# Loads of the matrices to be inverted: one DMA per 32 partitions in place of one per 64

## The chip, the cores and the metric

One core of one Trainium2 chip runs the kernel. The metric is the device time of one execution in microseconds (us); lower is better. Before the change the median of three runs is 1321.84 us.

## The reference, cut to what matters

A recurrence over 768 positions (32 pairs of batch and head, state 40 x 40), then two dense stages.

```python
for t in range(S):                                   # S = 768; B, H, D = 4, 8, 40
    y[:, :, t] = einsum('bhd,bhde->bhe', r[t], state)
    Sa = einsum('bhde,bhe->bhd', state, a[t])
    state = state * w[t] - Sa (x) b[t] + v[t] (x) k[t]
x = y as (3072, 320)
x = ((x @ w_a) * (x @ w_b)) @ w_out                  # 320 -> 1536 -> 320
each row of x to one of 8 experts (argmax of a gate): gate * relu(x @ w1[e]) @ w2[e]
```

## The kernel before, in words

The recurrence is worked in 12 chunks of 64 positions. Within a chunk the dependence of each position on the earlier ones is a triangular 64 x 64 matrix for each of the 32 pairs. Its two diagonal 32 x 32 blocks are inverted on VectorE (DVE): 64 small matrices, each held on two partitions (even and odd rows), so that all 128 partitions work at once. The off-diagonal block follows by small matmuls (`t21a`, `t21b`).

**The path of one inversion.** `scores` (L545) makes the matrices by matmuls (L551) of `ablk` and `bk`, ScalarE copies them to `s1` (L559), GpSimd masks them (L561), and SyncE (SP) writes them to a DRAM tile `nd` of shape [2, 32, 32, 32] (L568): diagonal block k, pair s, row j, column t. `tinv` (L602) loads them back into the tile `m` (L613 to L623): partitions 64k to 64k+31 and 64k+32 to 64k+63 get the same 32 matrices of 4 KB each. It then loads the identity into `xt` (L624) and returns 31 pairs of DVE steps, `mul` (L630) and `sub` (L636). At the last one `end` writes `xt` to a DRAM tile `td` (L647) and reads it back into `s1` (L651, L652).

**What sets the order.** PE, DVE, ScalarE and GpSimd run in the order in which the program is written. `phase1` goes through 24 slots for each chunk c and places work of the chunks c, c+1, c+2 and c+3 in them by the table `STEADY`. For chunk c+2: its `bk` is loaded in slot 0 (L471), its `a` in slot 2 (L521, multiplied on GpSimd at L523 and spread into `ablk` at L531), `bk` is scaled on DVE in slot 2 (L541), `scores` stand in slots 7, 8, 16 and 17, `tinv` is called in slot 22, and its DVE steps run in slots 2 to 16 of the next chunk. Slot 0 of a chunk also loads `rblk` (L725) and `r` (L729), which the matmuls at L826 and L844 use. The matmuls of the first dense layer (L1019, tile `pm`) for the chunk before are laid into the odd slots, 16 in each; their products (L1031) go out as `hT` (L1033). Steps that convert 64-bit weights (lines 365 to 388) are mixed between the steps of the inversion.

All these loads and stores are issued by SP, in one order. The loads of the 64-bit weights and of `v` are issued by ScalarE. DMAs of SP and ScalarE take turns with eight completion semaphores, so a DMA waits until the one eight earlier in the program's order has landed.

**Special cases.** The inversions of chunks 0 and 1 are made ahead of the loop. Chunk 1 has its tiles lent by another pool (`room`): there `m` is two halves of 16 rows, which are loaded apart (L616). The chunks 2 to 11 use L621.

Of the kernel before, what the change touches and what calls it, by code (L numbers as in the profile page):

```python
# [22 lines left out]
R = C // 2  # L23
# [109 lines left out]
def phase1(tc, I, cst, drm, psA, psM, ident, hT, mk_ident, wo, xs, span, tiny, down):  # L133
# [61 lines left out]
    while tinv or t1:  # L195
        both += tinv[:1] + t1[:1]
        tinv, t1 = tinv[1:], t1[1:]
# [202 lines left out]
def urow(b, o):  # L400
    return slice(C * (b % 2) + o, C * (b % 2) + o + R)


class Attention:
# [197 lines left out]
    def tinv(self, c, room=None):  # L602


        nc = self.nc
        st = self.st[c]
        if room:
            m, xt = room
        else:
            t = self.p1.tile([128, R, R], F32, tag="m", name=f"m{c}")  # L610
            m = [t[:, R // 2 * h:R // 2 * h + R // 2] for h in range(2)]
            xt = self.p1.tile([128, R // 2, R], F32, tag="xt", name=f"xt{c}")
        for k in range(2):  # L613
            if room:
                for h in range(2):
                    nc.sync.dma_start(  # L616
                        m[h][64 * k:64 * k + 64].rearrange("p j t -> p (j t)"),
                        st["nd"][k, :, R // 2 * h:R // 2 * h + R // 2].rearrange(
                            "s j t -> s (j t)")[None].to_broadcast([2, 32, R * R // 2]))
            else:  # L620
                nc.sync.dma_start(  # L621
                    t[64 * k:64 * k + 64],
                    st["nd"][k].rearrange("s j t -> s (j t)")[None].to_broadcast([2, 32, R * R]))  # L623
        nc.sync.dma_start(xt, self.I["one"].rearrange("p (i t) -> p i t", t=R))  # L624

        def mul(s, box):
            n, rows = R - 1 - s, s // 2 + 1
            tmp = self.p2.tile([128, 136], F32, tag="tmp", name=f"tmp{c}_{s}")[:, :rows * n]
            box.append(tmp.rearrange("p (i t) -> p i t", t=n))
            nc.vector.tensor_tensor(  # L630
                box[0], m[2 * s // R][:, s % (R // 2):s % (R // 2) + 1, s + 1:].to_broadcast([128, rows, n]),
                xt[:, :rows, s:s + 1].to_broadcast([128, rows, n]), op=ALU.mult)

        def sub(s, box):
            rows = s // 2 + 1
            nc.vector.tensor_tensor(  # L636
                xt[:, :rows, s + 1:], xt[:, :rows, s + 1:], box[0], op=ALU.subtract)
            if s == R - 2:
                end()

        def end():
            t0, t1 = self.td[c % 2]
            for k, t in ((0, t0), (1, t1[:, :, R:])):
                tv = t.rearrange("s (i k) t -> k s i t", k=2)
                for q in range(2):
                    p = 64 * k + 32 * q
                    nc.sync.dma_start(tv[q], xt[p:p + 32])  # L647
            for b in range(B):
                s1 = st["s1"][b // 2][:, b % 2]
                ss = slice(8 * b, 8 * b + 8)  # L650
                nc.sync.dma_start(s1[urow(b, 0), :, 0:R], t0[ss].rearrange("s j t -> j s t"))  # L651
                nc.sync.dma_start(s1[urow(b, R)], t1[ss].rearrange("s j t -> j s t"))  # L652

        out = []
        for s in range(R - 1):
            box = []
            out.append(lambda s=s, box=box: mul(s, box))
            out.append(lambda s=s, box=box: sub(s, box))
        return out
# [1122 lines left out]
```

## Time and profile before

| | |
|---|---|
| median of 3 runs | 1321.84 us (1315.72 to 1326.93) |
| the profiled execution: its own time | 1319.37 us |
| the profiled execution: span from first to last instruction | 1317.2 us |
| mean granted TensorE clock | 0.884 of full speed |
| busy: PE, DVE, ScalarE (ACT), GpSimd (POOL) | 1051.8, 704.1, 521.6, 439.3 us |

The span is one execution. Engines overlap, so busy times do not add up to it. "SPq" is the time that SP's queue takes to issue a DMA; when a DMA lands is seen in the chain of waits and in what waits for it. The recurrence runs to about 870 us, the rest is dense work.

### The profile page before, as it was taken

Reading aid. Unit: us, or ns where it says so; the run is one execution under the profiler, and the core shown is the slowest. Engines: PE = TensorE matmul, PEld = TensorE weight load, DVE = VectorE, ACT = ScalarE, POOL = GpSimd, SP = SyncE. Lnnn points to the kernel's source line nnn. Section 1 sums busy time; section 2 is a strip of 40 time slices with the busy share of each in tenths; the row PEclk is TensorE's granted clock in tenths of the full one; section 3 lists DMA queues with packets and bytes.
Section 4 is the critical chain, followed back from the end, with each engine's and each line's share of the span. In section 5 each row is a group of like instructions: output and inputs, shape, how many; then the busy total and the mean of one; then the engine's idle time right before and its main releaser. Section 6 shows DMA issues by size and latency. Waiting matters only on the chain.

```text
span 1317.2 us, 27177 instructions
## 1 busy us (share of the span) xinstructions
PE 1051.8 (80%) x10402; PEld 1005.3 (76%) x10402; DVE 704.1 (53%) x1843; ACT 521.6 (40%) x1229; POOL 439.3 (33%) x464
## 2 busy tenths in 40 slices
PE   2304649788786877779788889999999989999995
PEld 2303639687776866778787879899999989999995
DVE  7488648382846646283848383713366684222221
ACT  3435634343342524344343324343233434445441
POOL 5442533121322312122332222112022255666550
PEclk9655659889897879889897989999799999999998
DMA  7363344446564838454444433318255727454510
GB/s 189 92 163 77 87 100 101 110 100 136 126 120 122 158 105 155 112 133 116 116 102 117 100 89 91 90 53 232 81 175 174 237 82 226 135 161 146 156 44 13
DMA packets 236828, 162.21 MB, mean 123 GB/s; under 512 B 142594, under 2 KB 220115, under 8 KB 236689
## 3 DMA queue, kind: packets, MB, share of 16 engines
q1 hardware_dynamic: 218945, 133.15, 39.3%
q0 software_dynamic: 9808, 15.76, 4.2%
q10 hardware_dynamic: 7936, 11.47, 3.1%
q8 instruction: 84, 1.38, 0.4%
q14 instruction: 55, 0.45, 0.1%
HBM read 107.34 MB, written 44.60 MB: 115 GB/s over the span
## 4 chain that ended last, share of the span: by engine, by line
PE 39%; DMA 25%; DVE 17%; issue 8%; POOL 4%; ACT 4%; SPq 2%; ACTq 0%; POOLq 0%; DVEq 0%
PE pm L1019 10%; PE py L1156 8%; DMA m<-nd 8%; PE dn L1465 5%; PE u L1445 5%; DVE tmp L630 5%; DVE xt L636 4%; DMA wo<-wo 3%; DMA xt<-in_one 3%; DMA bk<-in_bk 2%; PE s1p L551 2%; DMA at<-in_a 2%; POOL s L833 2%; DMA out<-y,ids 1%; PE py L850 1%
## 5 line engine op out<-in xcount | busy, mean ns | idle before, releaser
L630 DVE TENSOR_TENSOR tmp<-m,xt 128x126 f32<-128x126 f32 (+22 forms) x372 | 127.6, 346 | 116.1 <-DMA bk<-in_bk 79.4
L1019 PE MATMUL pm<-xl,wh 128*128 128x256 f32 x576 | 134.7, 317 | 15.5 <-ACT ua L1022 13.2
L551 PE MATMUL s1p<-ablk,bk 120*128 120x192 f32 (+1 forms) x264 | 64.6, 400 | 92.3 <-DMA ablk<-at 58.7
L1031 DVE TENSOR_TENSOR uh<-pm,ua 128x256 f32<-128x256 f32 x144 | 60.5, 420 | 141.5 <-PE pm L1019 93.2
L551 PEld LDWEIGHTS s1p<-ablk,bk 120*128 120x128 f32 x264 | 57.1, 249 | 96.4 <-issue 77.7
L1019 PE MATMUL pm<-xh,wl 128*128 128x256 f32 x576 | 120.8, 293 | 0.0
L1019 PE MATMUL pm<-xh,wh 128*128 128x256 f32 x576 | 119.7, 291 | 0.0
L636 DVE TENSOR_TENSOR xt<-xt,tmp 128x126 f32<-128x126 f32 (+22 forms) x372 | 113.5, 308 | 8.2
L1448 DVE SCALAR_TENSOR_TENSOR hl<-u,hh 128x384 fp32r<-128x384 f32 (+5 forms) x72 | 41.5, 580 | 139.1 <-ACT hh L1447 139.1
L1019 PEld LDWEIGHTS pm<-xl,wh 128*128 128x128 f32 x576 | 93.7, 202 | 19.6 <-ACT ua L1022 14.0
L1019 PEld LDWEIGHTS pm<-xh,wl 128*128 128x128 f32 x576 | 94.7, 202 | 0.0
L1019 PEld LDWEIGHTS pm<-xh,wh 128*128 128x128 f32 x576 | 93.8, 200 | 0.0
L833 POOL TENSOR_SCALAR_AFFINE_SELECT s<-s 64x512 f32<-64x512 f32 x96 | 70.7, 737 | 67.6 <-ACT s L831 63.2
L1156 PE MATMUL py<-wl,hh 128*128 128x328 f32 x288 | 92.5, 321 | 0.6 <-DVE wl L1127 0.6
L1156 PE MATMUL py<-wh,hl 128*128 128x328 f32 x288 | 91.3, 317 | 2.0 <-DVE hl L1146 2.0
L1156 PE MATMUL py<-wh,hh 128*128 128x328 f32 x288 | 91.1, 316 | 0.0
L561 POOL TENSOR_SCALAR_AFFINE_SELECT s<-s 64x512 f32<-64x512 f32 x48 | 37.3, 778 | 150.1 <-ACT s L559 144.8
L826 PE MATMUL p<-rblk,uv 120*128 120x192 f32 (+1 forms) x288 | 61.3, 377 | 30.4 <-DMA rblk<-in_r 29.6
L1022 ACT COPY ua<-pm 128x256 f32<-128x256 f32 x144 | 53.7, 373 | 79.0 <-PE pm L1019 58.8
L1019 PE MATMUL pm<-xl,w 128*128 128x256 f32 x288 | 84.0, 292 | 0.0
L1019 PE MATMUL pm<-xh,w 128*128 128x256 f32 x288 | 83.9, 291 | 0.0
L826 PEld LDWEIGHTS p<-rblk,uv 120*128 120x128 f32 x288 | 58.0, 240 | 32.0 <-issue 31.0
(236 smaller groups left out, 2750.8 us busy)
## 6 DMA issues: line engine op xcount, KB each, us to landing
hT<-uh SPq DMA_DIRECT2D x72, 256.0 KB
hf<-hT SPq DMA_DIRECT2D x36, 512.0 KB
r<-in_moe_w SPq DMA_DIRECT2D x8, 1280.0 KB
r<-in_moe_w SPq DMA_DIRECT2D x8, 1024.0 KB
bk<-in_bk SPq DMA_DIRECT2D x11, 720.0 KB
xs<-zt SPq DMA_DIRECT2D x8, 805.0 KB
m<-nd SPq DMA_DIRECT2D x22, 256.0 KB
at<-in_a SPq DMA_DIRECT2D x24, 180.0 KB
```

The lines of the kernel that those rows point to most:

```text
L551: nc.tensor.matmul(ps[:2 * C, 3 * g * C:(3 * g + n) * C], st["bk5"](b, g), self.ablk[b // 2][:, b % 2, g, 0:n, 0:C], start=True, stop=True)
L630: nc.vector.tensor_tensor(box[0], m[2 * s // R][:, s % (R // 2):s % (R // 2) + 1, s + 1:].to_broadcast([128, rows, n]), xt[:, :rows, s:s + ...
L636: nc.vector.tensor_tensor(xt[:, :rows, s + 1:], xt[:, :rows, s + 1:], box[0], op=ALU.subtract)
L826: nc.tensor.matmul(p2[b][:, 3 * g * C:(3 * g + n) * C], self.cur[b]["uv"][:, 128 * g:128 * g + 128], self.rblk[:, b % 2, g, 0:n, 0:C], sta ...
L833: nc.gpsimd.affine_select(out=s2t[q * C:q * C + C], in_=s2t[q * C:q * C + C], pattern=[[0, 8], [1, C]], base=0, channel_multiplier=-1, com ...
L1019: nc.tensor.matmul(p, l, r, start=(i == 0), stop=(i == len(seq) - 1))
L1022: nc.scalar.copy(a, p)
L1031: nc.vector.tensor_tensor(h[:, f % 2], p, a, op=ALU.mult)
L1156: self.nc.tensor.matmul(py, self.pair[i][l][:, k, s], self.W[r][:, first + k, cols], start=(first + k == 0 and n == 0), stop=(first + k == ...
L1445: nc.tensor.matmul(p, l, r, start=(i == 0), stop=(i == len(seq) - 1))
L1448: nc.vector.scalar_tensor_tensor(out=hl, in0=p, scalar=0.0, in1=hh.bitcast(F32), op0=ALU.max, op1=ALU.subtract)
L1465: nc.tensor.matmul(p, l[:, q], r[:, f], start=(f == 0 and i == 0), stop=(f == len(hs) - 1 and i == 2))
```

## The change

For each diagonal block k, the DMA that filled 64 partitions reads its source through a leading broadcast dimension of 2, that is, as [2, 32, 1024] elements. It becomes two DMAs, q = 0 and 1, that fill 32 partitions each, whose source is [32, 32, 32] without a broadcast. The same bytes reach the same places. For the chunks with L621 there are four DMAs of 128 KB in place of two of 256 KB; for chunk 1 there are eight of 64 KB in place of four of 128 KB.

```diff
         for k in range(2):
-            if room:
-                for h in range(2):
-                    nc.sync.dma_start(
-                        m[h][64 * k:64 * k + 64].rearrange("p j t -> p (j t)"),
-                        st["nd"][k, :, R // 2 * h:R // 2 * h + R // 2].rearrange(
-                            "s j t -> s (j t)")[None].to_broadcast([2, 32, R * R // 2]))
-            else:
-                nc.sync.dma_start(
-                    t[64 * k:64 * k + 64],
-                    st["nd"][k].rearrange("s j t -> s (j t)")[None].to_broadcast([2, 32, R * R]))
+            for q in range(2):
+                p = slice(64 * k + 32 * q, 64 * k + 32 * q + 32)
+                for h in range(2 if room else 0):
+                    nc.sync.dma_start(m[h][p], st["nd"][k, :, R // 2 * h:R // 2 * h + R // 2])
+                if not room:
+                    nc.sync.dma_start(t[p], st["nd"][k])
         nc.sync.dma_start(xt, self.I["one"].rearrange("p (i t) -> p i t", t=R))
```

## Rows read from the trace of the kernel before

**Rows 1.** The page's 40 equal slices of the span: PE's busy tenths.
```profile
PE   2304649788786877779788889999999989999995
```

**Rows 2.** The chain that ended last, its shares of the span by line.
```profile
by line: PE pm L1019 10.2%; PE py L1156 7.8%; DMA m<-nd 7.6%; issue 7.5%; PE dn L1465 5.3%; PE u L1445 5.1%; DVE tmp L630 4.8%; DVE xt L636 3.7%; DMA wo<-wo 3.4%; DMA xt<-in_one 3.1%; DMA bk<-in_bk 2.2%; PE s1p L551 2.1%; DMA at<-in_a 1.6%;
```

**Rows 3.** DMA issues by tile: count and KB each.
```profile
m<-nd SPq DMA_DIRECT2D x22, 256.0 KB
...
m<-nd SPq DMA_DIRECT2D x4, 128.0 KB
```

**Rows 4.** The timeline of SP: start, us, line, what, count.
```profile
385.45 1.25 SPq L621 DMA_DIRECT2D m<-nd  x2
386.75 0.41 SPq L624 DMA_DIRECT2D xt<-in_one  x1
...
387.68 10.11 SPq L725 DMA_DIRECT2D rblk<-in_r  x3
397.89 1.05 SPq L729 DMA_DIRECT2D r<-in_r  x2
400.64 0.32 SPq L471 DMA_DIRECT2D bk<-in_bk  x1
...
426.70 1.24 SPq L725 DMA_DIRECT2D rblk<-in_r  x3
```

**Rows 5.** The chain in order of time, 380 to 415 us: start, us, what.
```profile
384.40 1.69 DMA nd<-s
...
386.16 14.42 DMA m<-nd
...
400.64 5.92 DMA bk<-in_bk
```

**Rows 6.** Busy time by stretch; last three columns: granted clock, DMA share, GB/s.
```profile
386.20:390.00 3.80, 3.80 (x68) 3.47 (x68) 1.41 (x4) 2.64 (x7) 0.00 (x0) 1.00 0.69 179
...
396.00:398.00 2.00, 2.00 (x18) 1.91 (x16) 0.00 (x0) 1.10 (x3) 0.00 (x0) 1.00 0.13 51
...
400.60:406.60 6.00, 3.75 (x12) 3.49 (x12) 0.21 (x2) 0.58 (x1) 0.00 (x0) 0.59 0.82 217
```

**Rows 7.** The timeline of PE, same boundary; in brackets idle time before.
```profile
402.76 3.75 PE L826 MATMUL p<-rblk,uv 120*128 120x192 f32 x12 [4.65 <-DMA rblk<-in_r]
412.94 2.05 PE L551 MATMUL s1p<-ablk,bk 120*128 120x192 f32 x6 [6.43 <-DVE tmp L630]
```

**Rows 8.** The timeline of SP at the first and last of eight such boundaries.
```profile
236.56 1.39 SPq L621 DMA_DIRECT2D m<-nd  x2
...
252.12 0.33 SPq L471 DMA_DIRECT2D bk<-in_bk  x1
...
738.00 1.28 SPq L621 DMA_DIRECT2D m<-nd  x2
...
753.85 0.33 SPq L471 DMA_DIRECT2D bk<-in_bk  x1
```

**Rows 9.** The timeline of PE after the last of them.
```profile
766.39 2.04 PE L551 MATMUL s1p<-ablk,bk 120*128 120x192 f32 x6 [6.32 <-DVE xt L636]
```

**Rows 10.** The timeline of SP at the inversions of chunks 0 and 1.
```profile
44.20 1.17 SPq L621 DMA_DIRECT2D m<-nd  x2
47.45 13.25 SPq L568 DMA_DIRECT2D nd<-s  x8
...
61.88 2.43 SPq L616 DMA_DIRECT2D m<-nd  x4
```

**Rows 11.** The timeline of DVE there.
```profile
59.98 0.19 DVE L630 TENSOR_TENSOR tmp<-m,xt 128x31 f32<-128x31 f32 x1 [13.15 <-DMA m<-nd]
...
75.57 0.38 DVE L630 TENSOR_TENSOR tmp<-m,xt 128x31 f32<-128x31 f32 x2 [4.81 <-DMA m<-nd]
```

**Rows 12.** The chain, 36 to 237 us: the load after the inversion of chunk 2.
```profile
164.54 16.82 DMA w<-in_w
```

**Rows 13.** Waits of SP, 120 to 870 us: us in total, times, longest.
```profile
SPq L568 <- DMA vn<-in_vn: 26.6, 9, 8.1
...
SPq L471 <- DMA m<-nd: 16.4, 9, 3.4
```

## The prediction

> **What bounds the kernel now.** I read the page's slices first, then the chain of waits, then the timelines of SP, PE and DVE around one load of `m`. In the slices PE stands at nine tenths from about the 25th on and mostly at six to eight tenths before [rows 1], so up to some 770 us something else sets the pace. The chain names it: `m<-nd` holds 7.6% of the span, 100 us, and `xt<-in_one`, which is issued right behind it, 3.1%, 41 us [rows 2]. For a load of 512 KB per inversion that is a lot. In the timeline of SP the two DMAs of one inversion are issued from 385.45 [rows 4]; in the chain the second lands 14.42 us after 386.16, whereas the larger `bk` (720 KB) needs 5.92 [rows 5]. The busy times say how the 14 us pass: at 396 to 398 the DMA engines are busy for a share of 0.13, about two of sixteen, at 51 GB/s, where the stretch after has 0.82 and 217 GB/s [rows 6]. Two engines carry the load and the other fourteen wait for work.
>
> What follows suffers too. SP issues `rblk` in three DMAs that take 10.11 us to issue, where the same three take 1.24 later in the chunk [rows 4]: SP is held up behind the full engines. `bk` then waits for `m` itself (nine such waits, 16.4 us in all [rows 13]), as each DMA waits for the one eight earlier. On PE this is 4.65 us of idle time before L826, for `rblk`, and 6.43 us before L551, the scores, which need `bk` and `ablk` [rows 7]. There are eight such boundaries, the first with `m` issued at 236.56, the last at 738.00 [rows 8]; after the last one's scores at 766.39 [rows 9] PE has no gap left to close.
>
> A rule of the Trainium skill ("DMA: Bandwidth & Descriptors", section "Rules for kernel authors") says that a DMA uses at most as many engines as its outermost dimension counts, and names a leading broadcast of c copies as the case that confines it to c; by it the old load has two engines and the new one, with 32 outermost, sixteen. The share of 0.13 agrees for the old load; no row shows the new form.
>
> **The change, part by part.** *Issues.* 22 DMAs become 44, and 4 become 8 [rows 3]: 26 more, at 1.25/2 = 0.62 us each [rows 4], two of them (1.25 us) on the path of an inversion.
>
> *The load itself.* No row shows its new form. Bounds for the landing after the last issue: 1.69 us from below, as the 32 KB of `nd<-s` take, and 14.42 from above, as now; the nearest is `bk` at 720 KB in 5.92 [rows 5], 122 GB/s with its fixed part, which gives 512/122 = 4.2 us. I take 4. It matters little: `m` is wanted by DVE together with `bk`, which comes later.
>
> *What is late next: `bk`.* SP after the first issue of `m` at 385.45: four issues 2.5, `xt` 0.4, one store of `hT` about the same, `rblk` 1.24 [rows 4], `r` 1.05 [rows 4], together 5.6 us, so 391.1. The wait for the DMA eight back now falls on `rblk`, `r` and `bk`, for the four parts of `m`; with a landing 4 us after 388.0 `bk` starts at 392.0 instead of 400.64, that is 8.6 us earlier. Behind that wait stand, on SP, `a` and then `ablk`, for which the scores wait; both move along with `bk`. From the issue of `bk` to the scores it is 412.94 - 400.64 = 12.3 us [rows 4, 7], and that stays. So the scores start at 404.3 instead of 412.94.
>
> *Whether PE is ready.* PE stopped at 402.76 - 4.65 = 398.1 before L826 [rows 7]; with `rblk` there it goes on at once, needs up to 3.75 us and is free at 401.9, still before 404.3. PE's gap shrinks from 11.1 to about 2.5 us, and DVE's steps of the inversion, which stand behind the scaling of `bk`, begin 8.6 us earlier as well. After the scores everything is relative to them, so the boundary's gain is kept.
>
> *The eight boundaries.* From the first issue of `m` to that of `bk` the first boundary takes 15.6 us, the last 15.9 [rows 8], this one 15.2 [rows 4]; the others lie between 14.3 and 15.9. With 6.6 us afterwards the gain is 7.7 to 9.3, 8.5 on average: 8 x 8.5 = 68 us. The load at 801 us belongs to the last inversion, past 766.39, where PE is the bound: 0.
>
> *Chunks 0 and 1.* `m` is issued at 44.20 [rows 10], and DVE is idle for 13.15 us until 59.98 and for 4.81 until 75.57 [rows 11]. With four issues (2.5) and a landing of 3 to 4 us the first start moves to about 50: 10 us won. The eight sends of `nd` behind it take 13.25 us to issue [rows 10]; freed, they end near 54, when chunk 1's scores are masked. Its eight loads take 8 x 0.6 = 4.9 us (2.43 for four [rows 10]) and land near 63. DVE, with its 10.8 us of steps between the two waits, is there at 61, so the second gap shrinks to 2. Together 12.5 us.
>
> *Chunk 2.* Behind its `m` the load of `w`, 366 KB, takes 16.82 us [rows 12], for which ScalarE, then DVE, then PE wait. Half of `bk`'s size should land within `bk`'s 5.92 [rows 5]; less 1.2 for the later issue, 16.8 - 5.9 - 1.2 = 9.7 are won, counted as 10.
>
> *The sum.* 68 + 12.5 + 10 = 90.5 us. The profiled execution took 1319.37 us (its span 1317.2 and 2.2 around it), 2.5 below the median shown and within its three runs: 1319.4 - 90.5 = 1229. A second way: the chain gives `m` and `xt` 141 us [rows 2]; with about 4.5 us left at each of eleven inversions, 141 - 50 = 91.
>
> **The rivals.**
>
> *The whole gap closes.* If `bk` comes sooner, PE's order is what is left: 4.65 + 6.43 = 11.1 us [rows 7] at eight boundaries, 89 us, and 25 for the start: 114 and 1205 us. For it: the 5.92 us of `bk` were measured in a stretch where DMAs had piled up (share 0.82 [rows 6]). Against: its successors pile up with it again.
>
> *The transfers only meet each other.* With `m` out of the way, `m`, `xt`, `hT`, `rblk`, `r` and `bk`, some 2.1 MB, want the engines at once. At the 179 GB/s of the first stretch [rows 6] they need 11.7 us and `bk` lands at 397.9, as forecast; at `bk`'s own 122 GB/s [rows 5] 17.2 us, so `bk` lands at 403.4 instead of 406.6: 3.2 us per boundary, 26, and half of the start, 11: 37 us and 1282. For it: the many short rows of `rblk`. Against: 217 GB/s in the busiest stretch [rows 6].
>
> *The load stays slow.* If what makes it slow is not the number of engines (all copies read the same 128 KB, say), it keeps its 14.4 us, and the added issues put 1.25 us on the path at ten inversions and 2.4 at chunk 1: 14.9 us and 1334, slower. It decides from a landing later than 386.16 + 14.42 - 385.45 = 15.1 us after the first issue [rows 4, 5], which is what the load takes now. Against: the share of 0.13 in DMA engines [rows 6], which a slow source would not confine to two of sixteen.
>
> The same page and section of the Trainium skill advises against splitting one transfer over disjoint halves of the partitions, since both spread over all sixteen engines and run one after the other; where that held for the old load, the change would only add issues, and the time would be that 1334. The 0.13 does not agree with it here.
>
> A wait for a DMA eight back can also hold SP on a transfer that ScalarE issues late: `vn` holds the sends of `nd` nine times, at most 8.1 us [rows 13]. These sends are ahead of `m`, and the two more DMAs come behind them, so I see no new one; each that arose would take up to 8.1 us off the gain at its boundary.
>
> **How the numbers follow.** The forecast of 1229 has a chance of 0.67, with 1212 to 1248 as its own range (7.5 to 10.5 us a boundary); the whole gap 0.12; the meeting transfers 0.14; the slow load 0.07. A measurement of this kernel, whose three runs lie 0.85% apart, tells about 1% from no change. Faster by over 1%: 0.67 + 0.12 + 0.13 = 0.92. Within 1%: half of the slow load and the rest of the third case, 0.05. Slower: 0.03. The range reaches from 1198, a little past the closed gap, to 1268, most of the way to the third case; the slow load and the tails beyond, 0.19 in all, are left out.
>
> **What would show it.** Right: `m<-nd` at 4 us or less in the chain, no stretch with a DMA share near 0.13 after it, three `rblk` issues in 1.3 us, `bk` issued about 6.6 us after the first `m`, idle time before L826 gone and before L551 at 2 to 4 us, and the last scores near 766 - 90 = 676 us. After these scores the remaining work takes as long as before. Wrong: `bk` landing later than 8 us after its issue (the transfers meet), or `m` still at 14 us. The forecast would also fail if the periods between scores were held by something that the load now hides, a chain through PE or ScalarE of less than 8 us of slack.

## The result and the profile after

The changed kernel takes 1227.7 us (median of four runs, 1226.58 to 1231.55) against 1321.9 us before (a median of four as well): a ratio of 0.9295, with a 95% interval of 0.925 to 0.934. The forecast was 1229. The execution that the profile shows took 1231.55 us, its span 1229.8; the mean granted clock is 0.915 (0.884 before).

The page's slices, PE's busy tenths:

```profile
PE   1404779988798887888999899999999999999995
```

PE stands at seven to nine tenths from the fifth slice on and mostly at nine from about the 20th, where it had six to eight for most of the way and nine only from about the 25th [rows 1]. The chain of the page, by line:

```profile
PE pm L1015 15%; PE py L1152 8%; PE u L1441 7%; PE dn L1461 7%; DVE tmp L626 5%; DMA wo<-wo 4%; DVE xt L632 4%; DMA hT<-uh 2%; POOL s L829 2%; PE s1p L551 2%; PE py L846 1%; DMA at<-in_a 1%; DVE bk L541 1%; PE p L822 1%; PE px L752 1%
```

`m<-nd` and `xt<-in_one`, 10.7% together in [rows 2], are no longer among the lines named, and `pm`, which stood at the head before too, goes from 10.2% to 15%. (In the changed kernel L617 and L619 load `m`; all lines past the change have moved up by four: L626 is the old L630, L721 the old L725, L822 the old L826.) The page counts 44 issues of `m` of 128 KB, as the change says.

SP at the boundary that answers to [rows 4], the first issues of `m` at the start, at chunk 2 (with the load of `w`) and at the first boundary, and the sends of chunk 1's `nd` (start, us, line, what, count):

```profile
44.96 2.06 SPq L619 DMA_DIRECT2D m<-nd  x4
...
50.02 6.00 SPq L568 DMA_DIRECT2D nd<-s  x8
...
57.32 6.46 SPq L617 DMA_DIRECT2D m<-nd  x8
...
152.55 1.01 SPq L619 DMA_DIRECT2D m<-nd  x2
154.13 0.34 SPq L462 DMA_DIRECT2D w<-in_w  x1
...
214.46 1.80 SPq L619 DMA_DIRECT2D m<-nd  x4
...
347.55 1.80 SPq L619 DMA_DIRECT2D m<-nd  x4
349.40 0.42 SPq L620 DMA_DIRECT2D xt<-in_one  x1
349.86 0.43 SPq L1029 DMA_DIRECT2D hT<-uh  x1
350.34 1.48 SPq L721 DMA_DIRECT2D rblk<-in_r  x3
351.91 0.93 SPq L725 DMA_DIRECT2D r<-in_r  x2
352.93 0.36 SPq L471 DMA_DIRECT2D bk<-in_bk  x1
```

The three issues of `rblk` take 1.48 us instead of 10.11, and `bk` goes out 5.4 us after `m` instead of 15.2. The load stands in the chain (start, us, what) at the inversion of chunk 0 alone. Before the change it took there, and after it takes:

```profile
44.84 15.04 DMA m<-nd
...
46.38 3.83 DMA m<-nd
```

At the eight boundaries it no longer stands in the chain, so that its landing there is seen only where something else waits for it. `r` does at two of them, 3.7 us in all (SP's waits are shown further below); at the longer one `r` is out 7.7 us after the first issue of `m`, where the old form had landed after 15.1 us [rows 4, 5].

Busy time by stretch at the same boundary (stretch, us, PE, PEld, DVE, ScalarE, GpSimd, then granted clock, DMA share, GB/s):

```profile
347.50:350.00 2.50, 2.50 (x48) 2.27 (x48) 0.58 (x2) 0.86 (x3) 1.00 (x1) 1.00 0.82 230
350.00:353.00 3.00, 3.00 (x62) 2.75 (x59) 0.61 (x2) 2.28 (x6) 0.00 (x0) 1.00 0.93 250
353.00:360.40 7.40, 7.40 (x140) 7.02 (x139) 0.52 (x2) 3.43 (x9) 0.00 (x0) 1.00 0.97 256
```

The stretch at 0.13 [rows 6] is gone: the engines are nearly full until `bk` has landed. ScalarE at the first use of chunk 2's `w`, and DVE, with the wait before it in brackets:

```profile
159.19 0.62 ACT L488 ACTIVATE junk<-w,wlim 120x384 f32<-120x384 f32 x1 [0.16 <-DMA w<-in_w]
```

```profile
51.41 0.19 DVE L626 TENSOR_TENSOR tmp<-m,xt 128x31 f32<-128x31 f32 x1 [3.87 <-DMA m<-nd]
...
65.02 0.40 DVE L626 TENSOR_TENSOR tmp<-m,xt 128x31 f32<-128x31 f32 x2
...
360.45 0.56 DVE L541 TENSOR_TENSOR bk<-bk,suf 120x384 f32<-120x384 f32 x1 [5.99 <-DMA bk<-in_bk]
```

`bk` was issued at 352.93 and is there at 360.4: 7.5 us, where it took 5.92 [rows 5]. PE at this boundary, and at the last scores:

```profile
362.11 1.91 PE L822 MATMUL p<-rblk,uv 120*128 120x192 f32 x12
366.14 1.11 PE L551 MATMUL s1p<-ablk,bk 120*128 120x192 f32 x6 [2.12 <-DMA ablk<-at]
...
681.80 1.11 PE L551 MATMUL s1p<-ablk,bk 120*128 120x192 f32 x6 [1.61 <-DMA ablk<-at]
```

The gap before `rblk`'s matmuls is gone, that before the scores is 2.12 us instead of 6.43 [rows 7], and the last scores start 84.6 us earlier than in [rows 9]. Here both groups of matmuls run at the full clock: 1.91 us for twelve and 1.11 for six, where it was 3.75 and 2.05 [rows 7]. By stretch, the two groups before the change, and both after it (columns as above):

```profile
402.76:406.51 3.75, 3.75 (x12) 3.46 (x12) 0.00 (x0) 0.58 (x1) 0.00 (x0) 0.50 0.96 258
412.94:414.99 2.05, 2.04 (x7) 2.05 (x8) 1.86 (x8) 0.00 (x0) 0.50 (x1) 0.50 0.77 172
...
362.11:367.25 5.14, 3.02 (x22) 2.86 (x21) 5.04 (x11) 1.50 (x3) 4.19 (x6) 1.00 0.26 60
```

The granted clock was 0.50 in both groups before, behind 4.65 and 6.43 us without a matmul, and is 1.00 now. That holds for `rblk`'s twelve at all eight boundaries (1.91 us). The scores' six take 1.11 us at four of them; at three they still take 2.04 to 2.05 us, behind gaps of 4.58 to 5.47 us, as here:

```profile
568.91 2.04 PE L551 MATMUL s1p<-ablk,bk 120*128 120x192 f32 x6 [5.47 <-DMA ablk<-at]
```

### The profile page after: what moved, and what is told of

It is laid out like the page before. It is cut to its first block, busy times and chain, and to the rows that moved or that the text cites. A ratio compares the mean times of both kernels' runs of the same rounds, so it can differ in the third digit from the quotient of the medians.

```text
span 1229.8 us, 27217 instructions
## 1 busy us (share of the span) xinstructions
PE 1035.7 (84%) x10402; PEld 991.2 (81%) x10402; DVE 703.1 (57%) x1843; ACT 523.0 (43%) x1229; POOL 439.1 (36%) x464
## 4 chain that ended last, share of the span: by engine, by line
PE 51%; DVE 18%; DMA 15%; issue 6%; ACT 4%; POOL 4%; SPq 1%; POOLq 0%; ACTq 0%; DVEq 0%
PE pm L1015 15%; PE py L1152 8%; PE u L1441 7%; PE dn L1461 7%; DVE tmp L626 5%; DMA wo<-wo 4%; DVE xt L632 4%; DMA hT<-uh 2%; POOL s L829 2%; PE s1p L551 2%; PE py L846 1%; DMA at<-in_a 1%; DVE bk L541 1%; PE p L822 1%; PE px L752 1%
## 5 line engine op out<-in xcount | busy, mean ns | idle before, releaser
L626 DVE TENSOR_TENSOR tmp<-m,xt 128x126 f32<-128x126 f32 (+22 forms) x372 | 126.3, 342 | 22.5 <-DMA rblk<-in_r 4.4
L551 PE MATMUL s1p<-ablk,bk 120*128 120x192 f32 (+1 forms) x264 | 59.8, 377 | 71.2 <-DMA ablk<-at 42.4
L551 PEld LDWEIGHTS s1p<-ablk,bk 120*128 120x128 f32 x264 | 52.7, 233 | 74.4 <-issue 50.4
L1205 POOL DMA_INDIRECT xs<-xr,si x24 | 28.0, 1168 | 138.5 <-DVE acc L1200 87.2
L994 POOL TENSOR_TENSOR xl<-xf,xh 128x384 fp32r<-128x384 f32 x24 | 24.3, 1011 | 144.8 <-ACT xh L993 121.2
```

Source lines behind the costliest of these rows:

```text
L551: nc.tensor.matmul(ps[:2 * C, 3 * g * C:(3 * g + n) * C], st["bk5"](b, g), self.ablk[b // 2][:, b % 2, g, 0:n, 0:C], start=True, stop=True)
L626: nc.vector.tensor_tensor(box[0], m[2 * s // R][:, s % (R // 2):s % (R // 2) + 1, s + 1:].to_broadcast([128, rows, n]), xt[:, :rows, s:s + ...
```

## The experiments

The theory (A): the old DMA is slow because it runs on two engines, as many as its outermost dimension counts; what is behind it is held up by those two full engines. Against it stand that the broadcast in the source, or the same 4 KB rows being read twice, made it slow, and that what was won came from another order of the queue and not from the engines. All ratios are against the kernel before on the same chip, with the 95% interval.

**The changed kernel once more**, as a measure for the others on the same chip.

> The changed kernel once more, unaltered, for comparison on the same chip with the three beside it: ratio 0.9295 (0.925 to 0.934) to the kernel before.

1226.27 us, a ratio of 0.9313 (0.928 to 0.935): the same gain in a second measurement.

**One engine, without a broadcast.** Each DMA of 32 partitions is cut into 31 and 1. There is no broadcast any more, and the bytes are the same.

```diff
             for q in range(2):
-                p = slice(64 * k + 32 * q, 64 * k + 32 * q + 32)
+                for s0, s1 in ((0, 31), (31, 32)):
+                    p = slice(64 * k + 32 * q + s0, 64 * k + 32 * q + s1)
...
-                    nc.sync.dma_start(t[p], st["nd"][k])
+                        nc.sync.dma_start(t[p], st["nd"][k, s0:s1])
```

> Each 32-partition load is cut into 31 and 1 partitions (eight DMAs per inversion, sixteen for chunk 1; same bytes). Theory A (the outermost count decides on how many DMA engines a load runs; a prime 31 leaves one): the load is slower than before, m lands some 25 to 29 us after its first issue against 15.1 before, a stretch behind it shows a DMA share near 1/16, and the kernel is slower than before: about 10 inversions x 12 us more, 1440 us (1380 to 1500). Theory B (it is the smaller parts, or more DMAs in flight, that made the load fast): like the changed kernel or a little above it, 1228 to 1245 us.

1419.7 us, 1.0805 (1.077 to 1.084), from two runs: slower than before the change, as theory A has it. SP at one boundary:

```profile
425.05 9.26 SPq L620 DMA_DIRECT2D m<-nd  x8
...
438.25 7.52 SPq L722 DMA_DIRECT2D rblk<-in_r  x3
...
448.88 0.36 SPq L471 DMA_DIRECT2D bk<-in_bk  x1
```

The load in the chain of the same kernel, and a microsecond of it in its busy times by stretch:

```profile
429.68 18.71 DMA m<-nd
```

```profile
442.00:443.00 1.00, 0.00 (x0) 0.00 (x0) 0.00 (x0) 0.00 (x0) 0.00 (x0) 0.82 0.06 25
```

A share of 0.06 is one engine of sixteen, at 25 GB/s; before it was 0.13, two, at 51 [rows 6]. So a load without any broadcast is slower than the old one, and runs on fewer engines. It lands 23.3 us after its first issue (25 to 29 were expected), and `bk` is issued 23.8 us after `m`. The Trainium skill says why 31 gives one engine ("DMA: Bandwidth & Descriptors", section "Why a DMA increments its semaphore by 16 and not by 1"): the count is the largest number up to 16 that divides the outermost sizes of both sides, so 31 leaves 1. The 0.06 agrees.

**Eight engines**: the same cut at 24 and 8 (`((0, 24), (24, 32))`), with the same number of DMAs as with 31 and 1.

> Each 32-partition load is cut into 24 and 8 partitions (eight DMAs per inversion, both counts divisible by 8; same bytes). Theory A (engines by the outermost count: eight): the load lands 2 to 4 us later than in the changed kernel, half of it by four more issues of 0.4 us and half by half the engines; bk goes out 1.5 to 3 us later at the eight boundaries: 1240 to 1252 us. Theory B (smaller parts are what counts): no slower than the changed kernel but for the issues, 1228 to 1240 us.

1236.12 us, 0.941 (0.939 to 0.943). SP:

```profile
352.82 2.77 SPq L620 DMA_DIRECT2D m<-nd  x8
...
359.34 0.51 SPq L471 DMA_DIRECT2D bk<-in_bk  x1
```

Two kernels with the same issues differ by 14% of the time before, by the place of the cut alone: 1.0805 and 0.941. That smaller parts are what helps is out by that. Eight engines against sixteen are not told apart: the ratio lies in the range that theory A gave (1240 to 1252 us are 0.938 to 0.947 of 1321.9), while the time itself lies in its rival's, as the kernel before takes only 1312.62 us on this chip. `bk` goes out 7.6 us after `m` on average, 1.5 later than in the changed kernel, and 1.0 of that is the four more issues of `m` (2.77 us against 1.80).

**One DMA per two groups kept, without the confinement.** `nd` holds the matrices twice, so that two DMAs of 64 partitions suffice, whose outermost dimension is 64. The price is twice the sends of `nd`.

```diff
-        st["nd"] = self.drm.tile([2, 32, R, R], F32, tag="nd", bufs=2, name=f"nd{c}")
+        st["nd"] = self.drm.tile([2, 64, R, R], F32, tag="nd", bufs=2, name=f"nd{c}")
...
+                    for q in range(2):
+                        s = 32 * q + 16 * pr + 8 * x
...
+            p = slice(64 * k, 64 * k + 64)
...
+                nc.sync.dma_start(t[p], st["nd"][k])
```

> nd holds each matrix twice (eight stores of 32 KB in place of four per pair of batches), and m is loaded as before the change by two DMAs of 64 partitions, whose source now counts 64 outermost without a broadcast. Theory A (the outermost count decides): m lands within 4 us as in the changed kernel, though there are no more loads than before the change; four more stores ahead of m cost about 1.8 us at each inversion: ratio 0.935 to 0.950. Theory B (the split into more and smaller DMAs is what helped): m keeps its 14 us and the kernel is as before or slower, ratio 1.0 to 1.02.

1257.72 us, 0.9577 (0.955 to 0.961), a little above what was expected, and far from the rival's 1.0. SP at the start and at the first boundary:

```profile
38.55 9.44 SPq L569 DMA_DIRECT2D nd<-s  x16
...
51.81 13.08 SPq L569 DMA_DIRECT2D nd<-s  x16
...
229.10 1.29 SPq L619 DMA_DIRECT2D m<-nd  x2
...
235.32 0.33 SPq L471 DMA_DIRECT2D bk<-in_bk  x1
```

From `m` to `bk` it is 6.2 us, as quick as after the change, with as many DMAs as before it. So it is the outermost dimension that counts, not the number of DMAs or their size. The doubled sends seem to cost more than thought: the first boundary comes at 229.1, not 214.5, and from the scores to the next `m`, where sends of `nd` stand too, the seven stretches take 332.9 us against 315.4. Together that is more than the 24.6 us by which the two spans differ. That it is the sends was not tried apart.

**One of the two diagonal blocks in the old form** (`k == 0` old, `k == 1` new).

```diff
+            wide = k == 0
+            for q in range(1 if wide else 2):
...
+                    if wide:
...
+                            v.rearrange("s j t -> s (j t)")[None].to_broadcast([2, 32, R * R // 2]))
```

> The old form for block k = 0, the new form for k = 1: half the bytes of m on two engines. Theory A (engines by the outermost count): the old half takes about half of what the whole took, m lands 8 to 9 us after its first issue, the issues of rblk stretch to some 4 us, bk goes out 8.5 to 10.5 us after the first m instead of 6.3, and a quarter to a half of the gain is lost: ratio to before 0.945 to 0.965. Rival (any DMA with the old form keeps its 14 us, because its time is a fixed cost and not bytes by engines): m lands 14 us after and the ratio is 0.985 to 1.0.

1272.4 us, 0.9668 (0.964 to 0.970): about half of the gain, just above the 0.945 to 0.965 that theory A gave and clear of its rival's 0.985. SP:

```profile
366.00 0.56 SPq L628 DMA_DIRECT2D m<-nd  x1
366.71 0.81 SPq L631 DMA_DIRECT2D m<-nd  x2
...
368.51 5.33 SPq L733 DMA_DIRECT2D rblk<-in_r  x3
...
378.00 0.37 SPq L471 DMA_DIRECT2D bk<-in_bk  x1
```

With one old DMA `rblk` takes 5.33 us to issue, between 1.48 (none) and 10.11 (two), and `bk` follows `m` by 12.0 us, between 5.4 and 15.2 (11 on average over the eight boundaries; 8.5 to 10.5 were expected). Two old DMAs add up: with both issued the share is 0.13 [rows 6], two engines and not four, so they share the same two.

**Where the gain lies: only chunks 0 and 1 in the new form** (`wide = c > 1`).

> The new loads for chunks 0 and 1 alone, the old ones for chunks 2 to 11. By the prediction's term 12.5 us won against before: 1309 us. By the profile after the change, where chunk 2's m goes out 10.5 us earlier: 1311 us. If the start's gain is made up for later by another wait (rival): 1317 to 1322 us.

1305.45 us, 0.9931 (0.991 to 0.996): 7.2 us won, less than expected, though the interval reaches to 12.5. In its profile chunk 2's `m` is issued at 151.37 and before at 162.98, which is 11.6 us, and behind it nothing is lost again (first boundary's `m` to last scores 528.6 us, 529.8 before). But these are two single executions, not side by side; the 7.2 us come from medians on one chip.

**Only the last inversion in the old form** (`wide = c == NCH - 1`).

> The old form for chunk 11 alone, whose m is issued after the last scores, where PE has no gaps. The prediction counts 0 there: like the changed kernel, within 0.3%. Rival (each inversion's load is worth the same 8 us, whatever PE does): 0.6% slower than the changed kernel.

1230.54 us, 0.9337 (0.931 to 0.936), against 0.9313 (0.928 to 0.935) for the changed kernel on the same chip. The intervals overlap, but 4 us lie between the medians. The last scores of this kernel start here, in a span of 1231.7 us:

```profile
682.47 1.11 PE L551 MATMUL s1p<-ablk,bk 120*128 120x192 f32 x6 [3.43 <-DMA ablk<-at]
```

and of the changed kernel on the same chip here, in a span of 1224.6 us:

```profile
675.65 1.11 PE L551 MATMUL s1p<-ablk,bk 120*128 120x192 f32 x6 [3.01 <-DVE xt L632]
```

Behind them the two need 549.2 and 549.0 us. In these two executions the old form costs nothing there; what they differ by arose ahead, where both kernels do the same.

**`bk` first.** If the load of `m` now only shares the engines with `bk`, then `bk`, for which the scores wait, should go ahead of it. The load of the next chunk's `bk` is moved from the first slot of a chunk to the end of the slot before, ahead of `m`, and for that the call that loads `m` goes from slot 22 to slot 23.

```diff
-                if i == T["load"]:
+                if i == T["load"] and c == 0:
                     A.load_bk(c2)
...
-            if i == T["inverse"] and c2 < NCH:
+            if i == 23 and c3 < NCH:
+                A.load_bk(c3)
+            if i == 23 and c2 < NCH:
```

> The changed kernel, with the next bk issued ahead of m and xt: load_bk moves from slot 0 to the end of slot 23 of the chunk before, and tinv's loads behind it. If bk and the a load behind it are now what the scores wait for at the eight boundaries (the changed profile has PE gaps of 1.6 to 5.5 us there, 26 us in all): bk lands 5 us earlier, the scores come 1 to 4 us earlier at each, 1205 us (1198 to 1218). Rival (the scores follow the a load, which stays where it was, or PE's own order): no change, 1224 to 1232 us.

1199.17 us, 0.9131 (0.911 to 0.916): within what was expected, the best version, and faster than both kernels. SP:

```profile
275.41 0.36 SPq L473 DMA_DIRECT2D bk<-in_bk  x1
275.89 2.75 SPq L621 DMA_DIRECT2D m<-nd  x4
...
279.64 3.25 SPq L723 DMA_DIRECT2D rblk<-in_r  x3
```

PE, at this boundary and at the last scores:

```profile
293.12 1.80 PE L553 MATMUL s1p<-ablk,bk 120*128 120x192 f32 x6 [4.12 <-DVE tmp L628]
...
650.76 1.11 PE L553 MATMUL s1p<-ablk,bk 120*128 120x192 f32 x6 [1.18 <-DMA ablk<-at]
```

From the first boundary's `m` (213.7) to the last scores it is 437.1 us, against 467.3 after the change (463.2 in its second profile). Of these 30 us only 11.9 lie at the eight boundaries: from `m` to the scores it is 16.5 to 18.7 us, against 17.7 to 20.5. The other 18.4 lie between the scores and the next `m`, where seven stretches take 297.0 us against 315.4. The reason given above does not explain that larger part; its cause is not shown.

**`bk` first with the old loads.**

> The kernel with bk first, but all loads of m in the old form. It parts what m costs by landing late itself from what it costs by holding bk behind it: bk is out of its way, but DVE's first step, rblk and the a load still stand behind m on two engines. If being late itself is what counts, the scores come some 23 us after m instead of 27, and the start wins nothing: ratio 0.965 to 0.990. Rival (only bk's place in the queue counted, so that the split isn't needed once bk is ahead): ratio 0.93 to 0.95.

1297.73 us, 0.9875 (0.985 to 0.991), as expected, though the scores come 25.3 us after `m` on average and not 23 (27.1 before). SP:

```profile
384.53 1.21 SPq L630 DMA_DIRECT2D m<-nd  x2
...
386.86 11.27 SPq L735 DMA_DIRECT2D rblk<-in_r  x3
...
400.96 0.33 SPq L523 DMA_DIRECT2D at<-in_a  x1
```

With `bk` out of its way the old load still holds SP for 11.27 us at `rblk`, and `a`, from which `ablk` is made, goes out 16.4 us after `m`. So the order of the queue was not what cost most of the time: it gives 1.25% with the old loads, and 1.6 to 1.8% on top of the new ones (0.9131 against 0.9295 and 0.9313).

**`bk` and half of `a` first.** With `bk` first and the new loads, PE waits for `ablk` at the last scores; so the load of half of `a` is moved ahead of `m` too. It needs a third buffer, for which `tmp` gives up one; DVE's steps are then laid in by two, and the table's `lead` is 6 instead of 5.

```diff
             if i == 23 and c3 < NCH:
                 A.load_bk(c3)
+                A.st[c3]["raw", 0] = A.load_a(c3, 0)
...
-        both += tinv[:1] + t1[:1]
-        tinv, t1 = tinv[1:], t1[1:]
+        both += tinv[:2] + t1[:2]
+        tinv, t1 = tinv[2:], t1[2:]
```

> As the run with bk first, and the a load of the first pair ahead as well (a third buffer for it; the buffer of tmp drops from two to one and the two inversions of the start alternate by pairs of steps, to make room). If the scores then wait for bk alone, which lands about 9 us after m's first issue, they come 1 to 3 us earlier at the eight boundaries than with bk first: ratio to before 0.897 to 0.908. Rival (PE's own order, or bk meeting m on the engines, is the bound): ratio 0.910 to 0.916, as with bk first.

1207.23 us, 0.9172 (0.915 to 0.920): a miss, no better than `bk` alone and above even what the rival gave (0.910 to 0.916). PE at the first boundary:

```profile
235.33 1.91 PE L828 MATMUL p<-rblk,uv 120*128 120x192 f32 x12
237.07 1.04 PE L557 MATMUL s1p<-ablk,bk 120*128 120x192 f32 x6
```

Hardly any idle time is left in front of the scores (at most 0.4 us at any of the eight boundaries): there PE's own order bounds, and an earlier `a` can give nothing more. From `m` to the scores the eight take 15.9 us less than with `bk` alone, but the seven stretches from the scores to the next `m` take 12.7 us more, so what a boundary gains isn't always kept. The first `m` is issued 5.7 us later (219.4), and behind the last scores it takes 548.6 us against 543.9. Whether the smaller `tmp`, the steps by two or the other `lead` makes the start later was not tried.

## Why the prediction was right

**Two engines carry the load.** Shown. The time follows the number of engines: 1.0805 with one, 1 with two, 0.941 with eight, 0.93 with sixteen (the last step is not told apart from the added issues). That a slow source keeps the load at 14.4 us, the rival on the other side, falls with the landing of 3.83 us, and by 31 and 1, where the broadcast goes and the load becomes slower. The advice of the Trainium skill ("DMA: Bandwidth & Descriptors", section "Rules for kernel authors") against splitting a transfer over two halves of the partitions rests on both halves using all sixteen engines; it doesn't hold for a DMA that is confined to two, as 0.9295 shows. The copy in `nd` shows that no split is needed, if the outermost dimension is large.

**The load itself.** Taken as 4 us, measured 3.83 at chunk 0; at two of the eight boundaries, where it meets other loads, it is late enough for `r` to wait for it. Four issues were put at 2.5 us and take 1.80.

**SP held up at `rblk`.** Taken to fall from 10.11 to 1.24 us; measured 1.48.

**`m` to `bk`.** Forecast 6.6 us; the eight boundaries have 5.4 to 7.8, 6.2 on average, where the old load had 14.3 to 15.9.

**`bk` to the scores.** This is the term that was mis-sized. "From the issue of `bk` to the scores it is 12.3 us, and that stays" holds only roughly: it is 11.3 to 14.1, 12.8 on average, where the eight boundaries had 12.0 before. `bk` now moves in a stretch where the engines are busy for 0.82 to 0.97, and from its issue to its first use on DVE it takes 5.7 to 7.9 us, 6.9 on average (5.9 before); the longest is just short of the 8 us that the prediction named as a sign of being wrong. At six of the eight boundaries the wait for the scores ends with `ablk`, whose `a` is loaded right behind `bk`. That is the rival of the meeting transfers, at 0.8 us a boundary instead of the 5.3 between its price and the forecast's (8.5 less 3.2). Where `bk` goes first, 1.2 to 1.8 us of the way from `m` to the scores come back.

**PE ready.** The first gap is gone, as forecast; that before the scores, put at 2.5 us, is 1.6 to 5.5, 3.3 on average. The rival of a closed gap did not come, as `bk` and `ablk` still end last; in the version with `bk` and half of `a` first it did.

**The sum**, by the starts of `m` and of the scores in the two profiles (chunk 2's `m` was issued at 162.98 before):

| stretch | before, us | after, us | gain | forecast |
|---|---|---|---|---|
| up to chunk 2's `m` | 162.98 | 152.55 | 10.4 | 12.5 |
| from there to the first boundary's `m` | 73.6 | 61.9 | 11.7 | 10 |
| eight boundaries, first `m` to last scores | 529.8 | 467.3 | 62.5 | 68 |
| from the last scores to the end | 550.8 | 548.0 | 2.8 | 0 |
| span | 1317.2 | 1229.8 | 87.4 | 90.5 |

At the start DVE begins at 51.41 and 65.02 where 50 and 63 were forecast. At chunk 2 the load of `w` is there 5.1 us after its issue (154.13, first use 159.19), where it took 16.82 [rows 12]. In the eight boundaries two errors partly cancel: the way from `m` to `bk` gave 71.2 us, more than the 68, the way from `bk` to the scores took 6.4 back, and the seven stretches from the scores to the next `m` another 2.3. That these stretches don't change, on which the boundaries' sum rests, held within that: 315.4 us after and 313.1 before. The last 2.8 us are smaller than the runs' own spread (5 us here) and are put down to nothing.

That 1229 and 1227.7 lie so close is in part luck. The profiled execution took 1231.55 us, the misses of the single terms have both signs, and the second profile of the changed kernel gives 13.1, 11.0, 66.6 and 1.9 us for the four rows, so that a term is known to about 4 us only. The last scores, looked for near 676, start at 681.80 in one and at 675.65 in the other.

New waits for an earlier DMA took little back. SP's waits from 110 to 780 us (us in total, times, longest), to be compared with [rows 13]:

```profile
SPq L568 <- DMA vn<-in_vn: 27.7, 8, 8.4
...
SPq L725 <- DMA m<-nd: 3.7, 2, 2.5
```

The waits for `vn` are as they were (26.6 us). The wait that `bk` had for `m` (16.4 us) now falls on `r`, as the prediction had it, and is 3.7 us at two boundaries.

## What to carry to other kernels

A DMA far slower than its bytes, in a stretch where the DMA engines' share is a few sixteenths, may be confined by its outermost dimension, as here: give both sides a large one (32 and 64 here), by splitting off a broadcast dimension or by a copy that has no broadcast, and put up with the added issues (0.45 us each here). Its price is looked for behind it, in issues that take eight times their usual (10.11 us against 1.24) and in loads that wait for its completion, as much as in its own wait. When such a load is quick, the engines are full where they were idle, and the order of the queue is next: what the critical engine waits for is worth trying first, and the whole time, not the boundary's gain, tells whether it pays.

## What was not expected

The DMA engines go from nearly empty for part of the boundary (0.13) to nearly full through it, 256 GB/s at a share of 0.97 up to `bk`'s landing. The forecast had taken 217 at 0.82 as the busiest rate; the trace before already had 258 at 0.96, in the stretch at 402.76 shown above.

PE's busy time falls from 1051.8 to 1035.7 us with the same number of matmuls, with a granted clock of 0.915 on average instead of 0.884. The scores' six took 2.05 us behind two gaps of 4.65 and 6.43 us, at 0.50 of the full clock, that is 1.2 of 2.4 GHz, and take 1.11 at 1.00 where the gap is 2.12; `rblk`'s twelve take 1.91 us everywhere. The forecast, which gave these "up to 3.75 us", had no term for it. In the stretches behind the scores it paid nothing that can be seen, since they are not shorter.
